# Linear attention and a squared-ReLU FFN on one core: q features scaled as token rows, moved by SBUF transfers, and x taken straight from the num product

## The chip, the cores and the metric

One core of a Trainium2 chip. The metric is device time in microseconds, as the median of several executions. Times of one comparison come from the same chip, with the kernel before run in the same rounds. TensorE multiplies matrices, VectorE and GpSimd work elementwise, ScalarE evaluates activations, SyncE issues transfers.

## The reference

```python
def _attn_ref(q, k, v, S1, S2):               # batch 4, heads 4, seq 1088, head_dim 32, r = 8
    def phi(x):
        a = np.einsum('rd,bhsd->bhsr', S1, x)
        b = np.einsum('rd,bhsd->bhsr', S2, x)
        return np.einsum('bhsi,bhsj->bhsij', a, b).reshape(*x.shape[:-1], r * r)
    q_p, k_p = (phi(q), phi(k))
    kv = np.einsum('bhsf,bhsd->bhfd', k_p, v)
    z = np.sum(k_p, axis=2)
    num = np.einsum('bhsf,bhfd->bhsd', q_p, kv)
    den = np.einsum('bhsf,bhf->bhs', q_p, z)[..., None] + 1e-06
    return (num / den).astype(np.float32)

def _moe_ref(x, w_in, w_out):                 # x: 4352 x 128, w_in: 128 x 2048
    h = np.maximum(x @ w_in, 0.0)
    return (h * h @ w_out).astype(np.float32)
```

## The kernel before

The FFN runs as one long stream on TensorE: 12 chunks (4 batches of 3, with 384, 384 and 320 tokens), each of 16 steps. A step is one f16 product (pg, 128 tokens of d_ff wide), a relu (gt) and a square (g) on ScalarE, VectorE or GpSimd, and one f32 product that accumulates in po. The attention of the next chunk is woven into this stream: a planner puts each small task into a step, and the tasks of a step are issued in that order on their engines, which work through their queues in order.

The k features of a batch are turned into token rows (fs) and multiplied with one another (kp), half on VectorE and half on GpSimd:

```python
    def a_fs(b, g):
        ...
            nc.vector.transpose(fs[:, 0 : 32 * n], kf[:, 0 : 32 * n])

    def a_kp2(b, g):
        fs = st[b, "fs", g]
        ...
        (nc.vector if g == 0 else nc.gpsimd).tensor_tensor(
            out=_ap(st[b, "kp2"], 0, 128, 128 * NT * g, [[64, 2 * NT], [8, 8], [1, 8]]),
            in0=_ap(fs, 0, 128, 0, [[16, 2 * NT], [2, 8], [0, 8]]),
            in1=_ap(fs, 0, 128, 1, [[16, 2 * NT], [0, 8], [2, 8]]),
            op=mult,
        )

    def k_tasks(n):
        for g in range(2):
            P.add(("fs", n, g), "DVE", 0.45, [("kf", n)], a_fs, n, g)
        ...
        for g in range(2):
            P.add(("kp", n, g), ("DVE", "POOL")[g], (1.36, 3.15)[g], [("fs", n, g)], a_kp2, n, g)
        turn_q(n, 0)
```

The q features of a chunk (a_qg) are spread by four VectorE shuffles and multiplied by GpSimd (qp). One group of products (a_ndn) makes num and den, and VectorE divides:

```python
    def a_ndn(b, ch):
        ...
        for i in range(2):               # num, den
            for g in range(2):
                for h in range(H):
                    nc.tensor.matmul(nd[32*h : 32*h+32, 512*g + 192*i : ...],
                                     kw[64*g : 64*g+64, 128*i + 32*h : ...], qpn[64*g : ...])
    # then: dT = transpose(den); de = dT + 1e-6; rd = 1 / de; rb = transpose(rd); x = num * rb
```

## Time and profile before

| | before |
|---|---|
| time, median of 3 runs | 195.05 us (194.82 to 195.51) |
| profiled span | 193.2 us |
| TensorE, ScalarE, VectorE, GpSimd busy | 96, 71, 64, 49% |
| first FFN product of po starts | 18.6 us |

In a page the busy share says how long an engine had something in flight; the slices show where. In a timeline the columns are start, length, engine, source line, operation and tiles; a bracket gives the idle time before it and who ended it. Two groups of the page are the halves of kp (count, then busy us, mean ns, idle before):

```profile
L306 POOL TENSOR_TENSOR kp<-fs 128x1152 f32<-128x1152 f32 x3 | 9.5, 3169 | 5.0 <-DVE fs L299 5.0
L306 DVE TENSOR_TENSOR kp<-fs 128x1152 f32<-128x1152 f32 x3 | 3.9, 1316 | 0.0
```

### The profile page before, as it was taken

How to read it: one execution, taken by the hardware profiler on the slowest of the kernel's cores; microseconds unless marked ns; L12 is line 12 of the kernel's file. 1: busy time of each engine (PE TensorE's matmuls, PEld its weight loads, DVE VectorE, ACT ScalarE, POOL GpSimd, SP SyncE). 2: the span in 40 equal slices, each digit the busy share in tenths (PEclk: the TensorE clock that was granted, in tenths of full speed). 3: DMA queues.
4: the chain of work that ended last, by engine and by line, in shares of the span. 5: the costliest groups of instructions: out<-in, count | busy, mean ns of one | idle time of the engine just before them, and what ended most of it. 6: DMA issues, size and time to landing. Idle time of an engine off the chain costs nothing.

```text
span 193.2 us, 4586 instructions
## 1 busy us (share of the span) xinstructions
PE 185.9 (96%) x1666; PEld 111.2 (58%) x1666; DVE 122.8 (64%) x316; ACT 138.1 (71%) x338; POOL 94.7 (49%) x158
## 2 busy tenths in 40 slices
PE   7998999999999999999999999999999999999990
PEld 2673655456656555456666555556566555556990
DVE  3958876974586763964566674873666665547740
ACT  3326695895496996996498896896596896867740
POOL 5833484955325382984346363984245371630000
PEclk9999999999999999999999999999999999999997
DMA  5699340020085100020157200010110200200201
GB/s 163 177 289 299 88 142 5 0 41 3 12 204 155 43 11 3 11 33 3 17 154 210 38 6 3 14 29 3 25 19 2 34 3 0 41 2 0 44 0 34
DMA packets 27344, 11.40 MB, mean 59 GB/s; under 512 B 19194, under 2 KB 26042, under 8 KB 27322
## 3 DMA queue, kind: packets, MB, share of 16 engines
q1 hardware_dynamic: 27174, 11.05, 23.5%
q8 instruction: 13, 0.21, 0.5%
q10 hardware_dynamic: 148, 0.07, 0.1%
q14 instruction: 9, 0.07, 0.1%
HBM read 8.78 MB, written 2.23 MB: 57 GB/s over the span
## 4 chain that ended last, share of the span: by engine, by line
PE 93%; DVE 2%; ACT 2%; issue 0%; DVEq 0%; ACTq 0%
PE po L756 58%; PE pg L725 16%; PE ndn L472 4%; PE kvp L338 2%; PE warm L877 2%; PE qg L441 2%; PE pt L773 2%; PE nd L595 2%; PE rep L901 1%; PE kvp L352 1%; PE sm L522 1%; PE kf L381 1%; PE kf L280 1%; ACT gt L735 1%; ACT g L719 1%
## 5 line engine op out<-in xcount | busy, mean ns | idle before, releaser
L756 PE MATMUL po<-g,w_o 128*128 128x384 f32 (+3 forms) x386 | 144.0, 459 | 0.0
L719 ACT ACTIVATE g<-gt 128x384 f32<-128x384 f32 (+1 forms) x164 | 80.7, 503 | 7.7 <-DVE gt L737 7.1
L735 ACT ACTIVATE gt<-pg 128x384 f32<-128x384 f32 (+2 forms) x137 | 64.6, 474 | 28.6 <-PE pg L725 27.9
L756 PEld LDWEIGHTS po<-g,w_o 128*128 128x128 f32 x386 | 65.9, 190 | 32.7 <-ACT g L719 18.7
L725 PE MATMUL pg<-xT,w_in 128*128 128x384 f16 (+2 forms) x193 | 60.9, 317 | 0.7 <-ACT xT L697 0.3
L737 DVE TENSOR_SCALAR gt<-pg 128x384 f32<-128x384 f32 (+1 forms) x56 | 29.4, 524 | 34.4 <-PE pg L725 27.9
L746 POOL TENSOR_TENSOR g<-gt 128x384 f32<-128x384 f32 (+1 forms) x26 | 20.7, 801 | 49.0 <-ACT gt L735 49.0
L725 PEld LDWEIGHTS <-w_in 128*128 128x128 f16 x193 | 18.9, 98 | 24.4 <-issue 6.8
L459 POOL TENSOR_TENSOR qp<-sh 128x384 f32<-128x384 f32 (+1 forms) x20 | 18.8, 948 | 7.9 <-DVE sh L450 7.9
L450 DVE STREAM_SHUFFLE sh<-qg 128x384 f32<-128x384 f32 (+1 forms) x40 | 20.4, 563 | 0.0
L546 POOL TENSOR_TENSOR xT<-x,rs 128x384 f16<-128x384 f32 (+1 forms) x10 | 9.5, 952 | 6.2 <-DVE rs L537 6.0
L306 POOL TENSOR_TENSOR kp<-fs 128x1152 f32<-128x1152 f32 x3 | 9.5, 3169 | 5.0 <-DVE fs L299 5.0
L537 DVE TENSOR_SCALAR rs<-sm 128x384 uint32<-128x384 uint32 (+1 forms) x10 | 5.3, 527 | 7.9 <-PE sm L522 7.9
L482 DVE STREAM_TRANSPOSE dT<-ndn 128x384 f32<-128x384 f32 (+1 forms) x10 | 5.5, 548 | 7.0 <-PE ndn L472 7.0
L788 POOL COPY br<-beta 32x3 f32<-32x3 f32 x32 | 5.9, 183 | 6.4 <-DVE beta L678 5.1
L472 PE MATMUL ndn<-qp,kw 64*32 64x192 f32 (+1 forms) x320 | 8.4, 318 | 0.0
L555 POOL TENSOR_TENSOR bt<-s 128x384 f32<-128x384 f32 (+1 forms) x10 | 7.9, 786 | 0.0
L472 PEld LDWEIGHTS ndn<-qp,kw 64*32 64x32 f32 x320 | 4.7, 106 | 4.9 <-issue 3.9
L364 POOL TENSOR_TENSOR ks<-kp 128x1024 f32<-128x1024 f32 x3 | 7.1, 2365 | 0.2
L877 PE MATMUL warm<-zero 128*128 128x512 f16 x16 | 5.7, 521 | 1.2 <-DVE zero L160 1.2
L338 PEld LDWEIGHTS kvp<-kp,vn 128*32 128x32 f32 x288 | 4.8, 110 | 2.7 <-issue 2.2
L274 DVE STREAM_TRANSPOSE qT<-qn 128x384 f32<-128x384 f32 (+1 forms) x12 | 6.3, 535 | 0.0
(119 smaller groups left out, 154.9 us busy)
## 6 DMA issues: line engine op xcount, KB each, us to landing
vn<-in_v_dram SPq DMA_DIRECT2D x32, 64.0 KB, 3.9
kn<-in_k_dram SPq DMA_DIRECT2D x3, 544.0 KB, 11.9
qn<-in_q_dram SPq DMA_DIRECT2D x3, 544.0 KB, 3.3
out_dram<-oT SPq DMA_DIRECT2D x24, 48.0 KB, 1.8
w_in<-in_moe_w_in_dram SPq DMA_DIRECT2D x2, 512.0 KB, 9.0
w_o<-in_moe_w_out_dram SPq DMA_DIRECT2D x2, 512.0 KB, 11.1
out_dram<-oT SPq DMA_DIRECT2D x12, 40.0 KB, 1.7
qn<-in_q_dram SPq DMA_DIRECT2D x2, 192.0 KB, 3.8
```

The lines of the kernel that those rows point to most:

```text
L306: (nc.vector if g == 0 else nc.gpsimd).tensor_tensor(out=_ap(st[b, "kp2"], 0, 128, 128 * NT * g, [[64, 2 * NT], [8, 8], [1, 8]]), in0=_ap( ...
L450: nc.vector.stream_shuffle(in_=_ap(st[b, "qg", ch], 0, 128, 0, [[512, 2], [1, n]]), out=_ap(t_, 0, 128, 0, [[n, 2], [1, n]]), mask=mask_q[ ...
L459: nc.gpsimd.tensor_tensor(out=qp[:, 0 : 2 * n], in0=st[b, "sh", ch, s, 0][:, 0 : 2 * n], in1=st[b, "sh", ch, s, 1][:, 0 : 2 * n], op=mult,)
L472: nc.tensor.matmul(nd[32 * h : 32 * h + 32, 512 * g + 192 * i : 512 * g + 192 * i + n], st[b, "kw"][64 * g : 64 * g + 64, 128 * i + 32 * h ...
L546: nc.gpsimd.tensor_tensor(out=st[b, "xT"][:, 384 * ch : 384 * ch + n], in0=st[b, "x", ch][:, 0:n], in1=st[b, "rs", ch][:, 0:n], op=mult,)
L719: nc.scalar.activation(dst, src, Square)
L725: nc.tensor.matmul(pg[:, c0:c1], w_in[:, 128 * c : 128 * c + 128], st[b, "xT"][:, 384 * ch + c0 : 384 * ch + c1],)
L735: nc.scalar.activation(gt[:, c0:c1], pg[:, c0:c1], Relu)
L737: nc.vector.tensor_scalar(out=gt[:, c0:c1], in0=pg[:, c0:c1], scalar1=0.0, scalar2=None, op0=amax)
L746: (nc.vector if on[1] == "DVE" else nc.gpsimd).tensor_tensor(out=g2[:, c0:c1], in0=gt[:, c0:c1], in1=gt[:, c0:c1], op=mult)
L756: nc.tensor.matmul(st["po", b, ch][:, c0:c1], w_o[:, 128 * c : 128 * c + 128], g2s[i][1][:, c0:c1], start=first, stop=(c == NFF - 1), skip ...
L877: nc.tensor.matmul(t_[:, 0:512], zero[:, 0:128], zero[:, :])
```

## The change

Its intent is to halve the num and den products on TensorE. The q features are turned into token rows, den is formed there, and one factor is scaled by 1/den, so that the num product gives x directly. Turned back, half of the feature rows lie on the wrong partitions and are moved by SBUF transfers. Since z is no longer multiplied on TensorE for these chunks, the ones products go and a gram product (a_gram) of the k features takes their place, for which fs gets a new layout. The core of the diff, with cuts marked:

```diff
     def a_fs(b, g):
...
-            nc.vector.transpose(fs[:, 0 : 32 * n], kf[:, 0 : 32 * n])
+            nc.vector.transpose(
+                _ap(st[b, "fs"], 0, 128, 2 * g, [[32, 2 * NT], [4, 8], [1, 2]]),
+                _ap(kf, 0, 128, 0, [[16, 2 * NT], [2, 8], [1, 2]]),
+            )
...
     def a_kp2(b, g):
...
-            in0=_ap(fs, 0, 128, 0, [[16, 2 * NT], [2, 8], [0, 8]]),
-            in1=_ap(fs, 0, 128, 1, [[16, 2 * NT], [0, 8], [2, 8]]),
+            in0=_ap(fs, 0, 128, 2 * g, [[32, 2 * NT], [4, 8], [0, 8]]),
+            in1=_ap(fs, 0, 128, 2 * g + 1, [[32, 2 * NT], [0, 8], [4, 8]]),
...
+    def a_qgy(b, ch, qg):
...
+        for r in range(2):
+            for g in range(2):
...
+                nc.tensor.matmul(qg[64 * g : 64 * g + 64, ...], sw[b % 2][64 * r : 64 * r + 64, :], ...)
...
+    def a_mv(b, ch, e):
...
+        for to, p_, c_, of, o_ in todo:
+            nc.sync.dma_start(_ap(to, p_, 32, c_, [[1, n]]), _ap(of, o_, 32, 0, [[1, n]]))
...
     def feature_tasks(b, ch):
...
+        P.add(("tq", b, ch), "DVE", 0.5, need, a_tq, b, ch)
...
+        P.add(("den", b, ch), "DVE", 1.1, [("tq", b, ch)], a_den, b, ch, lag=0)
+        for e in range(2):
+            P.add(("qp2", b, ch, e), "POOL", 1.05, [("den", b, ch)], a_qp2, b, ch, e)
+        for e in range(2):
+            P.add(("bk", b, ch, e), "DVE", 0.5, [("qp2", b, ch, e)], a_bk, b, ch, e)
+            P.add(("mv", b, ch, e), "SP", 0.0, [("bk", b, ch, e)], a_mv, b, ch, e)
+        P.at["mv", b, ch, 1] += 5
...
     def k_tasks(n):
...
-        for g in range(2):
-            P.add(("kp", n, g), ("DVE", "POOL")[g], (1.36, 3.15)[g], [("fs", n, g)], a_kp2, n, g)
-        turn_q(n, 0)
+        P.add(("kp", n, 1), "POOL", 3.15, [("fs", n, 1)], a_kp2, n, 1)
+        if n == 1:
+            x_tasks(0, 2)
+        P.add(("kp", n, 0), "DVE", 1.36, [("fs", n, 0)], a_kp2, n, 0, slow=n > 1 and 1.5)
```

## The prediction

> **What bounds the kernel now.** I read the page first, then the chain that ended last, then the longest waits, then the timeline of TensorE alone. From the page, busy shares and the slices:
>
> ```profile
> PE 185.9 (96%) x1666; PEld 111.2 (58%) x1666; DVE 122.8 (64%) x316; ACT 138.1 (71%) x338; POOL 94.7 (49%) x158
> ...
> PE   7998999999999999999999999999999999999990
> ...
> PE 93%; DVE 2%; ACT 2%; issue 0%; DVEq 0%; ACTq 0%
> ```
>
> TensorE is busy 96% of 193.2 us, at 90% or more in all slices from the fifth to the last but one, and 93% of the chain that ended last is its own work; no other engine passes 71%. A busy TensorE need not be a full one, so I checked its timeline. Columns: start, length, work.
>
> ```profile
> 104.61 0.70 PE L756 MATMUL po<-g,w_o 128*128 128x320 f32 x2
> 105.24 0.88 PE L472 MATMUL ndn<-qp,kw 64*32 64x192 f32 x32
> 105.91 0.48 PE L441 MATMUL qg<-qT,sqn 64*32 64x160 f32 x16
> 106.33 0.34 PE L725 MATMUL pg<-xT,w_in 128*128 128x384 f16 x1
> ...
> 114.63 0.81 PE L756 MATMUL po<-g,w_o 128*128 128x384 f32 x2
> 115.27 0.33 PE L725 MATMUL pg<-xT,w_in 128*128 128x384 f16 x1
> 115.44 0.81 PE L756 MATMUL po<-g,w_o 128*128 128x384 f32 x2
> ...
> 131.93 1.21 PE L338 MATMUL kvp<-kp,vn 128*32 128x64 f32 x72
> 132.95 0.29 PE L352 MATMUL kvp<-kp,ones 128*32 128x64 f32 x8
> 133.07 0.29 PE L352 MATMUL kvp<-ks,ones 128*32 128x64 f32 x8
> 133.29 0.34 PE L725 MATMUL pg<-xT,w_in 128*128 128x384 f16 x1
> ```
>
> I go by distances between starts, as lengths overlap. A full FFN step takes 115.44 - 114.63 = 0.81 us: 0.64 for the f32 product of 384 columns and 0.17 for the f16 one, that is 600 f32 columns a us and 2400 f16 ones. I walked all starts from 18.6 us to the end and subtracted these rates. Apart from the attention groups, under half a us is left over, around 177.6 to 179.2, where ScalarE is late. So TensorE is full, and the time follows **what is put into its queue**. The waits say the same: the longest belong to engines waiting for work.
>
> ```profile
> POOL g L746 <- ACT gt L735: 49.0, 21, 4.8
> ACT gt L735 <- PE pg L725: 27.9, 40, 1.8
> DVE gt L737 <- PE pg L725: 27.9, 45, 2.0
> ```
>
> The columns are total, count and longest in us. All three are slack on the other engines.
>
> **The Trainium skill.** (1) "TensorEngine Tiling (Array Packing)", section Available Configurations, lists 64x32 as 8 independent tiles and 64x64 as 4. The trace agrees on 64x32: 8 products of qg (192 columns each) take about the time of one, 192/600 = 0.32 us plus an edge. (2) Same page, Key Properties: changing the tiling mode, not just the tile, drains TensorE. The trace fits. Between an FFN po and the ndn start there is 105.24 - 104.61 = 0.63 us, where 320 columns need 0.53: 0.10 us of edge. Out of qg there is 106.33 - 105.91 = 0.42 where 160 columns need 0.27: 0.15 us. Between ndn and qg, both 64*32, the start distance is 0.67 for 2 x 0.32: only 0.03. So a change of mode costs 0.10 to 0.15 us. (3) "DMA: Bandwidth & Descriptors", section Anatomy of one DMA (written for the GpSimd path), puts the fixed cost at about 2.0 us; here, issued by SyncE, output writes of 48 KB land in 1.8 us. (4) "GPSIMD Engine Reference", section Key points, says that GpSimd cannot access PSUM (no run here shows it), which is why xs must leave GpSimd when x is read straight from the num product.
>
> **The change part by part, on TensorE.** Three batches (b = 1 to 3) of three chunks change: six of 192-column and three of 160-column halves. Batch 0 keeps its path.
>
> 1. Num and den products: 16 products a chunk (two rounds of eight tiles) become 8 (one round), as den is applied to the q features beforehand. Two rounds were 0.67 us (192) and 0.57 (160: 117.79 to 118.36), so half: 6 x 0.335 + 3 x 0.285 = **-2.8 us**.
> 2. The q feature product stays one round of the same columns, but is 4 products of 64x64 instead of 8 of 64x32. No column time changes, but by point (2) the num product and the q product no longer share a mode: 8 groups x 0.12 = **+1.0 us**. In two groups the k features (64*32) follow, another 2 x 0.12 = **+0.2**.
> 3. The first q product of batches 2 and 3 was a group of its own (122.38 po to 123.61 pg, 1.23 us, less 0.64 for po: 0.59, where the columns need 0.32). It now rides in another group: two groups' edges of 0.25, **-0.5 us**.
> 4. In the kv group the ones products (8 of 64 columns, two rounds, 0.34 with a tail of 0.12: 0.22) become 9 gram products of 32 columns spread over the column tiles. If each stands alone, 9 x 32/600 = 0.48, so +0.26 a batch; if they hide beside the kv products, -0.2. I take +0.13 x 3 = **+0.4 us**.
> 5. Transposes of kv: batch 0's pair (0.22 us) moves to before the FFN stream begins, where TensorE waits for the first x behind warm-up products; some 0.1 of it may come back there. One of two goes in later batches, but a small product with a mask takes its place. Sum **-0.2 us**.
> 6. The |x| sum splits into two products of 192: 9 x 0.02, **+0.2 us**.
> 7. The last chunk leaves its output-tile products out of steps 0, 1, 6, 11 instead of the first four, which spreads the 0.4 us of lateness at 177.6: **-0.3 us**.
>
> Sum: -2.8 + 1.2 - 0.5 + 0.4 - 0.2 + 0.2 - 0.3 = -2.0 us.
>
> **Off TensorE.** A changed chunk loses on VectorE four shuffles (4 x 0.563), dT 0.548, de and rd 0.59, rb 0.54 and x 0.518: 4.4 us. It gains a turn of the features (about 0.54), four small operations for den (estimate 0.2 to 0.3 each from de and rd, 1.0), two turns back (1.08) and xs (0.52): 3.1 us. So 1.3 us less, 9 times, 12 us of VectorE. GpSimd loses qpn (2 x 0.948) and xs (0.952) a chunk and the ks sums (2.365 + 2 x 1.003 a batch) and gains two products of about 1.0 each: 0.8 a chunk and 4.4 a batch, about 20 us. None of this bounds the span, so its worth is near 0 by itself; it gives the FFN evictions more room. Six SBUF transfers a chunk are added, 54 in all, each 32 rows of 1.5 KB = 48 KB. Their latency lies between the turn back and the num product; the schedule leaves five extra steps plus the usual two, 7 x 0.81 = 5.7 us, against an estimate of 2 to 3 us after the output writes of the same size. I add **+0.4 us** for stalls where they queue behind loads of the next batch (landing 3.3 to 11.9 us in the page) or where a late VectorE turn eats the margin. Total -1.6; 195.05 - 1.6 = 193.4. As this kernel's stream has been kept free of stalls with care and the new schedule spreads its work evenly, I lean a little to the good side: **193.0 us**.
>
> **Rivals.**
> A. *The mode change costs nothing between 64x32 and 64x64* (or only the entry and exit count). Then the 1.2 us stay won: 191.8 us. For it: the 0.03 us between ndn and qg shows groups can run on seamlessly. Against: the 0.10 and 0.15 at both edges of every group.
> B. *The transfers become a new wait on TensorE.* Its queue is in order, so a num product waiting on a late transfer holds the whole FFN. One us in half of the nine chunks gives 4 to 5 us: 197 to 198. For it: one queue carries loads, outputs and moves, in order; the first chunk of batch 1 has the longest chain (k features, kv, gram, q, turn, product, turn back, move). Against: 5.7 us of room.
> C. *VectorE becomes the bound locally*: the new schedule lets it be loaded to 1.25 us a step everywhere where 0.99 held before, and the small den operations come in bursts. For it: an FFN step is only 0.81 us, so late relus would stall po. Against: its total falls by 12 us. It would cost 1 to 2 us: 194 to 195.
> D. *Everything off TensorE is hidden and nothing was on the path*: if the gram and the mode changes are worth more than I take, 194 to 195, no change.
>
> **Range and chances.** Summing the certain gain (2.8 + 0.5 + 0.5) with nothing against it gives 191.3, which I take as the low end. All costs at their high end (1.5 for modes, 0.8 for gram, 1.5 of stalls) against the gains give about 195. More than 2% faster means below 191.1 us, beyond the column arithmetic: 0.12. Slower than 199 needs rival B in most chunks: 0.04. The rest is 0.84.
>
> **What would show each step.** In the changed trace: the num product should have 16 instructions of 64*32 and a start distance of 0.33 us plus an edge; the q product, 64*64, should start 0.10 to 0.15 us later than the columns of num alone need (step 2; if 0.03, rival A). The kv group with its grams should take 1.4 to 1.7 us from po's end to the next pg (1.45 now). The gap at 177.6 should shrink. VectorE should fall to about 110 us and GpSimd to about 75, less what the FFN is given from ScalarE. Rival B would show as TensorE idle before ndn ended by a DMA; rival C as idle before po ended by VectorE. The prediction is wrong if those waits sum to over 2 us, or if the packed products do not share the array as they do now.

## The result and the profile after

The changed kernel takes 201.61 us (200.76 to 203.14, 4 runs) against 195.13 us for the kernel before in the same rounds. The ratio is 1.034, with a 95% interval from 1.027 to 1.041. Ratios here are the mean time of one kernel's fast runs over that of the other's fast runs of the same rounds, so not quite the ratio of the medians. A run over 1.5% above the fastest of the same kernel counts as slow. The page after:

```profile
PE 186.3 (94%) x1468; PEld 108.4 (54%) x1468; DVE 123.5 (62%) x284; ACT 130.6 (66%) x322; POOL 85.0 (43%) x166
...
PE   7997999899999699999999599999999999999990
...
PEclk9999999999999999999999879999999999999999
...
PE 77%; DVE 9%; issue 4%; DMA 3%; ACT 2%; SPq 2%; POOL 1%; ACTq 0%; DVEq 0%
```

TensorE has holes in the slices from 35, 65 and 110 us (8, 6 and 5; a slice is 5.0 us), and of the chain that ended last its share fell from 93 to 77%. To see where 6.0 us of span went, I split the time after the first po by the distances between the starts of all matmuls. "FFN columns" are the columns of pg, po and pt at 2400 and 600 a us. "Attention" is the distance from each attention matmul to the next one. "Rest" is what the FFN matmuls took beyond their columns: edges of groups (0.10 us each), a few ns per product, and waits. The row doesn't add up to the span: 5.2 us before and 5.6 us after lie behind the start of the last matmul.

| profiled run | first po | FFN columns | attention | rest | span |
|---|---|---|---|---|---|
| before | 18.6 | 144.5 | 20.6 | 4.3 | 193.2 |
| changed | 18.3 | 144.5 | 20.1 | 10.8 | 199.2 |

So attention on TensorE shrank and the FFN stream now waits. The single steps that lose over 0.25 us are few: 1.4 us near 35 us, 2.0 at 65.6, 2.4 at 109.3, and 1.4 in slow products up to 116.5. A num product at 153.6 waits 0.4 us for a transfer. Here is the timeline of the third of them:

```profile
106.76 2.71 POOL L361 TENSOR_TENSOR kp<-fs 128x1152 f32<-128x1152 f32 x1
...
107.16 4.36 DVE L361 TENSOR_TENSOR kp<-fs 128x1152 f32<-128x1152 f32 x1
...
109.24 0.49 ACT L918 ACTIVATE gt<-pg 128x384 f32<-128x384 f32 x1
...
111.42 0.56 DVE L920 TENSOR_SCALAR gt<-pg 128x384 f32<-128x384 f32 x1
...
112.04 0.32 PE L908 MATMUL pg<-xT,w_in 128*128 128x384 f16 x1 [2.25 <-DVE gt L920]
```

VectorE's half of kp, 1.32 us before, is recorded as 4.36 us. It starts 0.40 us after GpSimd's half and ends 2.05 us after that one has ended. The next relu (gt) stands behind it in VectorE's queue, and TensorE waits 2.25 us for that relu. In the kernel before the order was the other way about:

```profile
119.93 1.32 DVE L306 TENSOR_TENSOR kp<-fs 128x1152 f32<-128x1152 f32 x1
120.08 3.19 POOL L306 TENSOR_TENSOR kp<-fs 128x1152 f32<-128x1152 f32 x1 [1.38 <-DVE fs L299]
```

VectorE started first, and GpSimd's half, which nobody was waiting for, ended 2.02 us after VectorE's. The hole near 35 us has the same neighbour, but a tiny instruction on VectorE:

```profile
31.43 2.70 POOL L361 TENSOR_TENSOR kp<-fs 128x1152 f32<-128x1152 f32 x1 [1.31 <-DVE fs L352]
31.78 2.38 DVE L668 TENSOR_SCALAR de<-dT 128x10 f32<-128x10 f32 x1
...
35.40 2.21 DVE L361 TENSOR_TENSOR kp<-fs 128x1152 f32<-128x1152 f32 x1
35.51 0.56 ACT L693 ACTIVATE ax<-x,tiny 128x320 bf16<-128x320 f32 x1 [1.43 <-DVE x L684]
36.12 0.30 PE L701 MATMUL sm<-ax,part 128*128 128x320 bf16 x1 [0.78 <-ACT ax L693]
```

Adding 1e-6 to 10 columns lasts 2.38 us, until GpSimd's kp ends; x, ax and sm follow late, and ScalarE, which stands at ax, does no relus meanwhile. The kp at 35.40, with GpSimd idle, takes 2.21 us: dearer than 1.32 even alone. After the 2.25 us hole TensorE is slow for a while, as the granted clock by stretch shows (after the stretch come busy us and count of TensorE, weight loads, VectorE, ScalarE and GpSimd, then the clock, the DMA share and GB/s):

```profile
109.80:112.00 2.20, 0.00 (x0) 0.00 (x0) 2.20 (x3) 0.00 (x0) 0.00 (x0) 1.00 0.19 45
112.00:113.30 1.30, 1.26 (x5) 0.80 (x5) 1.21 (x3) 0.97 (x3) 0.00 (x0) 1.00 0.00 0
113.30:117.10 3.80, 3.80 (x30) 1.37 (x29) 0.71 (x2) 0.87 (x2) 0.83 (x1) 0.55 0.31 47
```

The clock is 0.55 for 3.8 us, which costs 3.8 x 0.45 = 1.7 us (an estimate from this row). Most of the loss doesn't need it: another of the four runs of the changed kernel had a mean clock of 0.997, where a stretch like this one alone would lower it to 0.991 (1 - 1.7/199), and still took 200.76 us. The 2.0 us hole near 65 us was followed by no low clock.

**Theories.** LOCK: a product of two SBUF tensors, or a short SBUF operation like de, on VectorE can't run beside a GpSimd instruction that reads SBUF; the later one waits for the whole of the other, and the wait is counted as its length. The Trainium skill says so in "SBUF — State Buffer", section SBUF: two separate sides: the pair of ports that the two share is "an exclusive lock, not a bandwidth split", and who starts first has it for the whole instruction. It names two kinds of VectorE operation: those with two SBUF inputs, against a GpSimd operation that reads SBUF (kp is one), and those in what it calls a 2-port perf mode. That de runs in such a mode is an inference; the runs show only that it waited. The traces above agree with the lock (2.05 us and 2.02 us left after the other's end). LAYOUT: kp reads one element in every 16 bytes instead of every 8. The same page, section Specifications (TRN2), gives SBUF lines of 16 bytes of which at least two hits are needed for full bandwidth; 2.21 against 1.32 us would fit. The rivals: TRANSFERS (the new SBUF moves), and COST (kp's own work, with no lock).

### The profile page after: what moved, and what is told of

The parts are those of the page before. It is cut to its first block, busy times and chain, and to the rows that moved or that the text cites. A ratio compares the mean times of both kernels' runs of the same rounds, so it can differ in the third digit from the quotient of the medians.

```text
span 199.2 us, 4283 instructions
## 1 busy us (share of the span) xinstructions
PE 186.3 (94%) x1468; PEld 108.4 (54%) x1468; DVE 123.5 (62%) x284; ACT 130.6 (66%) x322; POOL 85.0 (43%) x166
## 3 DMA queue, kind: packets, MB, share of 16 engines
HBM read 8.80 MB, written 2.23 MB: 55 GB/s over the span
## 4 chain that ended last, share of the span: by engine, by line
PE 77%; DVE 9%; issue 4%; DMA 3%; ACT 2%; SPq 2%; POOL 1%; ACTq 0%; DVEq 0%
PE po L939 48%; PE pg L908 13%; PE kvp L393 3%; PE ndn L637 2%; PE qk L564 2%; PE pt L956 2%; SPq L141 2%; PE nd L778 2%; DMA kn<-in_k_dram 1%; PE rep L1084 1%; DVE de L668 1%; ACT gt L918 1%; DMA ft<-ft 1%; DMA vn<-in_v_dram 1%; DVE fs L352 1%
## 5 line engine op out<-in xcount | busy, mean ns | idle before, releaser
L939 PEld LDWEIGHTS po<-g,w_o 128*128 128x128 f32 x386 | 65.9, 191 | 37.9 <-issue 20.1
L902 ACT ACTIVATE g<-gt 128x384 f32<-128x384 f32 (+1 forms) x146 | 72.2, 506 | 10.4 <-DVE gt L920 10.0
L929 POOL TENSOR_TENSOR g<-gt 128x384 f32<-128x384 f32 (+1 forms) x44 | 34.4, 789 | 57.9 <-ACT gt L918 57.8
L908 PEld LDWEIGHTS <-w_in 128*128 128x128 f16 x193 | 19.2, 99 | 22.9 <-issue 5.1
L599 POOL TENSOR_TENSOR qp<-tq,bs 128x384 f32<-128x384 f32 (+1 forms) x18 | 14.2, 810 | 16.9 <-DVE bs L591 16.9
L573 DVE STREAM_TRANSPOSE tq<-qk 128x384 f32<-128x384 f32 (+1 forms) x9 | 5.0, 561 | 13.7 <-PE qk L564 8.7
L361 DVE TENSOR_TENSOR kp<-fs 128x1152 f32<-128x1152 f32 x3 | 10.9, 3636 | 0.0
L985 DVE SCALAR_TENSOR_TENSOR sc<-po,bt 128x384 f32<-128x384 f32 (+1 forms) x9 | 4.8, 528 | 6.4 <-PE po L939 6.3
L720 DVE TENSOR_SCALAR rs<-ndn 128x384 uint32<-128x384 uint32 (+1 forms) x9 | 4.8, 536 | 3.7 <-PE ndn L704 3.5
L393 PE MATMUL kvp<-kp,vn 128*32 128x64 f32 x288 | 6.5, 223 | 0.0
L956 PE MATMUL pt<-w_o,g 128*128 128x128 f32 x32 | 5.7, 274 | 0.0
L637 PE MATMUL ndn<-ft,kw 64*32 64x192 f32 (+1 forms) x144 | 5.6, 347 | 0.0
```

Of the source, the lines that this page charges most:

```text
L361: (nc.vector if g == 0 else nc.gpsimd).tensor_tensor(out=_ap(st[b, "kp2"], 0, 128, 128 * NT * g, [[64, 2 * NT], [8, 8], [1, 8]]), in0=_ap( ...
L393: nc.tensor.matmul(st[b, "kvp"][32 * h : 32 * h + 32, 0:64], _ap(vn[b], 0, n, v0 + dv * h, [[1, 32]]), kp[0:n, at[h] : at[h] + 64], start= ...
L599: nc.gpsimd.tensor_tensor(out=_ap(qp, 0, 128, 0, [[32, m], [8, 4], [1, 8]]), in0=_ap(st[b, "tq", ch], 0, 128, 4 * e, [[32, m], [1, 4], [0, ...
L637: nc.tensor.matmul(nd[32 * h : 32 * h + 32, 512 * g : 512 * g + n], st[b, "kw"][64 * g : 64 * g + 64, 32 * h : 32 * h + 32], st[b, ch, "ft ...
L902: nc.scalar.activation(dst, src, Square)
L908: nc.tensor.matmul(pg[:, c0:c1], w_in[:, 128 * c : 128 * c + 128], st[b, "xT"][:, 384 * ch + c0 : 384 * ch + c1],)
```

## The experiments

Ten kernels ran, all correct. The first four shared one set of runs of the kernel before (195.4 us), the next four another (195.17 us), the last two a third (195.14 us). One run each of e3, e5 and e8 was slow; it is in the median given, but not in the ratio.

**e1: VectorE's half first.**

```diff
-        P.add(("kp", n, 1), "POOL", 3.15, [("fs", n, 1)], a_kp2, n, 1)
+        P.fix(("kp", n, 0), "DVE", 1.36, P.at["fs", n, 1], a_kp2, n, 0)
+        P.add(("kp", n, 1), "POOL", 3.15, [("fs", n, 1)], a_kp2, n, 1)
         if n == 1:
             x_tasks(0, 2)
-        P.add(("kp", n, 0), "DVE", 1.36, [("fs", n, 0)], a_kp2, n, 0, slow=n > 1 and 1.5)
```

> The changed kernel with one order undone: VectorE's half of the k products (kp) is queued right after the turn fs, ahead of GpSimd's half, as in the kernel before. In the changed kernel GpSimd's half starts first (2.70 us) and VectorE's half, begun 0.40 us later, lasts 4.34 us. Theory LOCK (a product of two SBUF tensors on VectorE waits for the whole of a GpSimd instruction that reads SBUF): VectorE's kp falls to about 2.2 us, GpSimd's kp grows to about 4.5, the stalls of TensorE near 65 and 109 us (2.0 and 2.4 us, and the low clock after the second) go; about 196 us. Rival TRANSFERS (the new SBUF moves hold things up): no change, 201 to 202. Rival COST (kp is slow by itself from its new layout): VectorE's kp stays near 4.3 us and the time at 201.

Measured: 204.23 us, ratio 1.045 (1.038 to 1.052). Slower, where every theory had said 196 or no change. The timeline of batch 1:

```profile
31.99 2.23 DVE L361 TENSOR_TENSOR kp<-fs 128x1152 f32<-128x1152 f32 x1
32.15 4.62 POOL L361 TENSOR_TENSOR kp<-fs 128x1152 f32<-128x1152 f32 x1 [1.31 <-DVE fs L352]
...
34.69 2.11 DVE L668 TENSOR_SCALAR de<-dT 128x10 f32<-128x10 f32 x1
...
38.77 0.42 PE L701 MATMUL sm<-ax,part 128*128 128x320 bf16 x1 [2.70 <-ACT ax L693]
```

The durations are those of LOCK: 2.23 us on VectorE, 4.62 on GpSimd, where 2.70 was its own. But the wait was only handed on. GpSimd's kp now ends at 36.8 instead of 34.1 us, de waits for it again (2.11 us), and sm comes 2.65 us later than in the changed kernel, with the 2.2 us of kp ahead of it; TensorE idles 2.7 us there and then runs at clock 0.50 for 6.3 us (38.77 to 45.09), which costs some 3.2 us (an estimate, half of 6.3). In batches 2 and 3 VectorE's kp meets another GpSimd product (2.73 us), and the x of the running chunk waits behind it (1.9 and 1.4 us). So the order of the two halves alone is no cure; the time forecast of LOCK was wrong, its durations were right.

**e2: 8 byte step.** The order of all instructions is unchanged; only fs stores the two factors in separate halves.

```diff
-                _ap(st[b, "fs"], 0, 128, 2 * g, [[32, 2 * NT], [4, 8], [1, 2]]),
-                _ap(kf, 0, 128, 0, [[16, 2 * NT], [2, 8], [1, 2]]),
+                _ap(st[b, "fs"], 0, 128, g, [[2, 16 * NT], [32 * NT, 2]]),
+                _ap(kf, 0, 128, 0, [[2, 16 * NT], [1, 2]]),
...
-            in0=_ap(fs, 0, 128, 2 * g, [[32, 2 * NT], [4, 8], [0, 8]]),
-            in1=_ap(fs, 0, 128, 2 * g + 1, [[32, 2 * NT], [0, 8], [4, 8]]),
+            in0=_ap(fs, 0, 128, g, [[16, 2 * NT], [2, 8], [0, 8]]),
+            in1=_ap(fs, 0, 128, 32 * NT + g, [[16, 2 * NT], [0, 8], [2, 8]]),
```

(a_gram reads the two halves as contiguous columns.)

> The changed kernel with only the layout of the k features altered, so that each kp reads with a step of 8 bytes as before instead of 16; the order of all instructions is the same. Theory LOCK plus LAYOUT: VectorE's kp without a GpSimd neighbour (batch 1) falls from 2.2 to 1.3 us; with one, from 4.34 to about 3 (the rest of a shorter GpSimd kp of about 2.0, then 1.3); the stalls shrink but do not go; about 197 us. LOCK alone: kp unchanged, 201 to 202. Rival COST (layout alone): kp 1.3 us everywhere and about 194.5. Rival TRANSFERS: no change in time.

Measured: 199.33 us, ratio 1.017 (1.010 to 1.025): slower than the kernel before, but whether by 2% is unclear. The instructions of kp (least, median and most ns):

```profile
L361 POOL TENSOR_TENSOR kp<-fs x3: 2274/2275/2282, 33.9 to 108.1; 128x1152 f32<-128x1152 f32 x3
L361 DVE TENSOR_TENSOR kp<-fs x3: 1348/3094/3099, 37.5 to 108.5; 128x1152 f32<-128x1152 f32 x3
```

Alone, VectorE's half is back at 1.35 us; GpSimd's fell from 2.70 to 2.28; beside GpSimd VectorE's still lasts 3.09. So LAYOUT and LOCK are both there, and COST alone (1.3 us everywhere) falls. The gain of 2.3 us over the changed kernel was half of what the 197 us expected would have been.

**e3: both edits.** Together, the edits of e1 and e2.

> The changed kernel with both: VectorE's kp first and the 8 byte step. LOCK plus LAYOUT: kp 1.3 us on VectorE, about 3.2 on GpSimd, as in the kernel before; the idle of TensorE at the FFN falls from 10.4 us to about 4 (3.3 in the kernel before), and the smaller attention share (20.8 against 22.4 us) shows: 193 to 195 us, near the 193.0 predicted. If transfers are the cause, it stays above 199.

Measured: 201.57 us, ratio 1.028 (1.020 to 1.036), a miss. Its profiled run fell in the slow state, so I read only durations from it: VectorE's kp 1.33 us in batch 1, then de 1.71 us behind GpSimd's, and 1.68 us for VectorE's kp in the other two batches. They fit the reason found in e1; with no fast trace that isn't shown. (The expectation's 10.4, 3.3, 20.8 and 22.4 us come from another way of splitting than the table above.)

**e4: both halves on GpSimd**, in the same places of the plan.

```diff
-        (nc.vector if g == 0 else nc.gpsimd).tensor_tensor(
+        nc.gpsimd.tensor_tensor(
```

> The changed kernel with both halves of kp on GpSimd, in the same places of the plan; VectorE gets none. All other instructions keep their order. LOCK: VectorE loses 10.9 us of kp and the stalls near 65 and 109 us go, though GpSimd's second half is done no sooner (2 x 2.7 = 5.4 us, about when VectorE's is done now); the one at 34 us ([...]de, behind GpSimd's kp) stays: 195 to 196.5 us. If kp's late result were what hurts (kv waiting for it), no change: 201. Rival TRANSFERS: no change.

Measured: 196.28 us, ratio 1.004 (0.998 to 1.010). The holes at 65 and 109 us are gone, that at 35 stays, as LOCK said; the rest falls from 10.8 to 5.9 us. The transfers are all still there, so TRANSFERS can't be what made the change slow.

**e5: the two halves one after the other**, by a real dependence: VectorE writes an element that GpSimd's half then overwrites.

```diff
+        if g == 0:
+            nc.vector.memset(st[b, "kp2"][:, 128 * NT : 128 * NT + 1], 0.0)
...
-        P.add(("kp", n, 1), "POOL", 3.15, [("fs", n, 1)], a_kp2, n, 1)
         if n == 1:
             x_tasks(0, 2)
         P.add(("kp", n, 0), "DVE", 1.36, [("fs", n, 0)], a_kp2, n, 0, slow=n > 1 and 1.5)
+        P.add(("kp", n, 1), "POOL", 3.15, [("kp", n, 0)], a_kp2, n, 1, lag=0)
```

> The changed kernel, 16 byte step kept, but GpSimd's half of kp is made to follow VectorE's by a real dependence (VectorE writes one element of GpSimd's output, which GpSimd then overwrites), so the two never overlap and the short operation de of batch 1 meets no GpSimd kp either. LOCK: VectorE's kp 2.2 us in all three batches, GpSimd's 2.7, de about 0.2 us instead of 2.4; the stalls of TensorE near 35, 66 and 109 us shrink to well under 1 us each; 195 to 197 us. If the lock is not the cause and kp's work as such is, the stalls stay near 2 us and the time above 199.

Measured: 196.18 us (fast runs 195.27 to 196.65), ratio 1.000 (0.992 to 1.008).

```profile
L361 DVE TENSOR_TENSOR kp<-fs x3: 2210/2245/2247, 33.8 to 105.1; 128x1152 f32<-128x1152 f32 x3
L361 POOL TENSOR_TENSOR kp<-fs x3: 2696/2697/2702, 36.2 to 107.4; 128x1152 f32<-128x1152 f32 x3
...
L670 DVE TENSOR_SCALAR de<-dT x1: 175/175/175, 32.4 to 32.4; 128x10 f32<-128x10 f32 x1
```

The work, the layout and the transfers are those of the changed kernel (the plan moved a few relus between engines), and kp has its plain durations in all three batches; de took 0.18 us. Taking away the overlap of the two engines takes away the 3.4%, to within the 0.8% of the interval. The rest falls from 10.8 to 4.8 us. Attention rises to 21.0 us, since two num products wait 1.5 us for transfers.

**e6: the lock in the kernel before.** One swap in each batch, so that GpSimd's half starts first.

```diff
-        for g in range(2):
-            P.add(("kp", n, g), ("DVE", "POOL")[g], (1.36, 3.15)[g], [("fs", n, g)], a_kp2, n, g)
-        turn_q(n, 0)
+        P.add(("kp", n, 1), "POOL", 3.15, [("fs", n, 1)], a_kp2, n, 1)
+        turn_q(n, 0)
+        P.add(("kp", n, 0), "DVE", 1.36, [("fs", n, 0)], a_kp2, n, 0, first=P.at["qT", n, 0])
```

> The kernel BEFORE with one swap in each of batches 1 to 3: VectorE turns q (0.57 us) ahead of its half of kp instead of after, so that GpSimd's half, which needs no more than fs, starts first. Everything else, the 8 byte step too, is as before. LOCK: VectorE's kp grows from 1.32 us to about 2.9 (the rest of a 2.0 us kp on GpSimd, then 1.3), GpSimd's shrinks from 3.17 to about 2.0 (it waited for VectorE before); the kernel gets slower by 0.5 to 4 us as relus queue behind kp. Without a lock both durations stay and the time is 195.

Measured: 196.79 us, ratio 1.0065 (1.001 to 1.012).

```profile
L306 POOL TENSOR_TENSOR kp<-fs x3: 2165/2165/2167, 32.5 to 120.7; 128x1152 f32<-128x1152 f32 x3
L306 DVE TENSOR_TENSOR kp<-fs x3: 2745/3074/3077, 33.1 to 121.0; 128x1152 f32<-128x1152 f32 x3
```

The lengths change places: GpSimd 3.17 to 2.17, VectorE 1.32 to 3.07. None of the change is in this kernel, so the lock is the chip's and not the change's. The cost in time is small: this trace has two holes of about 0.5 us where the changed kernel has three of 1.4 to 2.4. Why they are shorter was not tested.

**e7: the changed kernel repaired.** Both halves on GpSimd (e4), the 8 byte step (e2), and in batch 0's third chunk 1e-6 is added while den is read from PSUM, in place of de.

```diff
-        nc.vector.transpose(_ap(dT, ...), _ap(st[b, "nd", ch], 0, 128, 192, [[512, 2], [1, n]]))
+        nc.vector.tensor_scalar(out=_ap(dn, ...), in0=_ap(st[b, "nd", ch], 0, 128, 192, [[512, 2], [1, n]]),
+                                scalar1=1e-6, scalar2=None, op0=add)
+        nc.vector.transpose(dT[:, 0 : 2 * n], dn[:, 0 : 2 * n])
```

> The changed kernel with both halves of kp on GpSimd, the 8 byte step, and the den of batch 0's third chunk with its 1e-6 added while it is read from PSUM (so de, which waited 2.4 us for GpSimd, is gone). LOCK plus LAYOUT: GpSimd's kp 2.0 us each, no VectorE instruction over 0.8 us beside it, the stall near 35 us gone; idle at the FFN back to some 4.3 us as in the kernel before; 193 to 194.5 us. If it stays at 196, something else of the change costs.

Measured: 195.63 us, ratio 1.001 (0.994 to 1.008), above the 193 to 194.5 expected. GpSimd's halves took 2.28 us each. The rest is 4.29 us, as in the kernel before, and the hole at 35 us is gone. Yet the time only equals the kernel before. Its num products of two chunks took 0.81 and 1.12 us instead of 0.48, waiting for transfers: 1.0 us. The first po came 0.4 us later than in the kernel before, with no cause that I could show.

**e8: the q product in the num product's mode.**

```diff
-            for g in range(2):
-                c0 = 384 * ch + n * g
+            for o in range(4):
+                c0 = 384 * ch + n * (o // 2)
                 nc.tensor.matmul(
-                    qg[64 * g : 64 * g + 64, 512 * r : 512 * r + n],
-                    sw[b % 2][64 * r : 64 * r + 64, :],
+                    qg[32 * o : 32 * o + 32, 512 * r : 512 * r + n],
+                    sw[b % 2][64 * r : 64 * r + 64, 32 * (o % 2) : 32 * (o % 2) + 32],
```

> The same repaired kernel with the q feature product as 8 products of 64x32 instead of 4 of 64x64, so that it shares its tiling mode with the num product before it and the k features after it. MODE CHANGE (0.12 to 0.14 us each, 8 + 2 of them): 1.2 us less, 192 to 193 us, and the num product's distance to the q product falls from 0.48 to about 0.35 us. Rival A of the prediction (a change between these two modes is free): no difference.

Measured: 194.39 us (fast runs 193.5 to 194.72), ratio 0.993 (0.987 to 0.999), above the 192 to 193 expected. A group of TensorE in the changed kernel, then the same in this one:

```profile
56.03 0.56 PE L637 MATMUL ndn<-ft,kw 64*32 64x192 f32 x16
56.52 0.56 PE L564 MATMUL qk<-qT,sw 64*64 64x192 f32 x8
57.01 0.72 PE L431 MATMUL qk<-kq,sk 64*32 64x288 f32 x16
```

```profile
55.31 0.56 PE L637 MATMUL ndn<-ft,kw 64*32 64x192 f32 x16
55.66 0.53 PE L564 MATMUL qk<-qT,sw 64*32 64x192 f32 x16
55.98 0.69 PE L431 MATMUL qk<-kq,sk 64*32 64x288 f32 x16
```

From start to start 0.49 became 0.35 and 0.49 became 0.32, with twice the instructions in the q product. By these distances the ten changes of mode cost 8 x 0.14 + 2 x 0.17 = 1.5 us. Attention on TensorE fell from 19.97 us in e7 to 18.79, by the 1.2 us expected; it would have been 1.5, but two num products of this trace wait for transfers, some 1.3 us in all against 1.0 in e7. Rival A of the prediction falls. One of these two shows why they wait:

```profile
61.60 1.15 SPq L626 DMA_DIRECT2D ft<-ft  x2
62.88 3.71 SPq L626 DMA_DIRECT2D ft<-u  x4
...
67.36 1.10 PE L637 MATMUL ndn<-ft,kw 64*32 64x192 f32 x12
68.12 0.34 PE L564 MATMUL qk<-qT,sw 64*32 64x160 f32 x4
```

The moves themselves land in 1.9 us in the median and 2.7 at most here. But SyncE issues the six of a chunk one after the other, and from the first issue to the last it takes 3.1 to 4.5 us in this trace (4.5 for this chunk). With the landing that is 5.0 to 6.4 us. Why some single issues take 1.5 us where the median is 0.54 was not tested.

**e10: e8 again in five rounds.**

> The repaired kernel with the 64x32 q product once more, in five rounds, to narrow the interval against the kernel before (0.9929, from 0.9865 to 0.9993, in three rounds): the traces say 1.5 us less (191.7 against 193.2 us of span), so a ratio of 0.990 to 0.995.

Measured: 194.3 us (193.01 to 195.19), ratio 0.995 (0.992 to 0.998), at the upper edge of what was expected. The spread of over 2 us would fit waits for transfers that come and go (in this trace two num products still waited); with one trace that isn't shown.

**e9: two more steps for the transfers.**

```diff
-        P.at["mv", b, ch, 1] += 5
+        P.at["mv", b, ch, 1] += 5 if (b, ch) == (1, 0) else 7
```

> The same with the num product planned two steps later behind the transfers, 7 steps instead of 5 for all chunks but the first of batch 1 (which has no room). In the repaired kernels the num products of two chunks still waited for a transfer, 0.4 and 0.3 us in one trace, 0.3 and 0.6 in the other. If those waits are the transfers alone, they go and the time falls by about 0.7 us; if not, other work of the plan moves and it stays within 0.5 us of the run beside it.

Measured: 192.1 us (191.99 to 193.41), ratio 0.986 (0.984 to 0.988): below the kernel before by 1.4%, clear of the interval though less than 2%, and by 2.2 us below e10 beside it, more than the 0.7 expected. No num product waits in its trace: each takes 0.35 us at 192 columns before a q product, and attention is 17.4 us, 1.6 less than in e10's trace. The profiled run, 193.41 us, lost some 1.2 us to half-speed products between 19.1 and 21.7 us, which is about what sets it off from the other runs at 192. What the plan moved besides the num products was not separated.

## Why the prediction was wrong

193.0 us was predicted, in a range of 191.3 to 195; 201.61 was measured. By its own steps:

- **What bounds the kernel** was right for the kernel before: TensorE is full, and the FFN columns stay at 144.5 us in every trace. One reading was too low: apart from attention not "under half a us" but 4.3 us is left over before, 1.7 of it in edges and 2.6 in a few ns per product; only 0.3 us is a wait. The miss doesn't come from there.
- **Step 1**, -2.8 us: held. In e8's trace the num products that don't wait take 0.35 and 0.30 us, where they were 0.67 and 0.57 with den: 6 x 0.32 + 3 x 0.27 = 2.7.
- **Step 2**, +1.2 us for changes of mode: held in kind and a little low; the distances in e7 and e8 give 1.5.
- **Step 3**, -0.5 us: the two separate q groups are gone from the trace.
- **Step 4**, +0.4 us: too high. The kv group takes 1.38 us (39.37 to 40.75) with the grams, 1.37 us before, so they add nothing beside the kv products.
- **Steps 5 and 6**: near, -0.1 and 0.0 us. **Step 7**, -0.3: the lateness at the last chunk is gone.
- **The step that failed** is "I add +0.4 us for stalls", in the part off TensorE. In the changed trace the stalls are some 7.6 us (1.4 + 2.0 + 2.4 + 1.4 + 0.4), 5.8 us of them behind VectorE operations that waited for GpSimd. The prediction's own sign of being wrong, such waits of over 2 us in sum, came true: 4.1 us of idle before pg ended by VectorE (it had named po). The mechanism of these stalls was missing too: the list of what VectorE and GpSimd gain and lose left out kp, which the diff shows twice, once with a new step and once with the halves in the other order. "About 12 us of VectorE" saved came out as 0.7 us more busy time: kp grew from 3.9 to 10.9 us and de by 2.2, mostly waits for GpSimd, which are counted as busy. The 12 was too much by itself, though: e5, without these waits, has 118.4 us, 4.4 less than before, and of the gap only the slower layout of kp (2.8 us) is traced.
- **Rival C** (VectorE the local bound, 1 to 2 us) named the right engine and the wrong reason: not the bursts of small operations, but a queue held up by another engine. **Rival B** (transfers) was real at a tenth of its size in the changed kernel, 0.4 us, and 1.0 to 1.6 us in e5, e7, e8 and e10. The estimate of 2 to 3 us against 5.7 us of room counted the landing of one transfer and not the six issues in a row: 5.0 to 6.4 us in e8's trace.

The 6 us between the two kernels are thus the lock with the longer kp behind it, and, in the profiled run, the clock that falls after the longest hole. e5 shows that taking away the overlap takes away the loss. What the layout alone costs is the step from the changed kernel to e2, about 2 us, measured with the lock in force. The low clock is the 1.7 us estimated above; no experiment isolated it, and the run of 200.76 us went without it.

## What to carry to other kernels

When a change reorders elementwise work, list every instruction of VectorE and GpSimd that may run side by side, and ask which starts first: an instruction that nobody waits for may hold one that the whole pipeline stands behind. An instruction whose recorded length varies with its neighbour, like the 3.17 us of GpSimd's kp before, is a warning to be read before predicting. Keep neighbouring groups of small matmuls in one tiling mode even at twice the instructions, and when several transfers feed one product, add up their issues on the queue, here six of 0.5 to 1.7 us each, and not only the landing of one.

## What the Trainium skill lacked or had wrong

- "SBUF — State Buffer" has the lock but not that a profile counts the wait as length of the waiter: a 10-column operation of 0.18 us was recorded as 2.38 us, a 1.32 us product as 3.07.
- The same page speaks of a penalty but gives no cost for VectorE with one hit in a 16 byte line: the product of 1152 elements rose from 1.35 to 2.21 us there.
- "TensorEngine Tiling (Array Packing)" says that a change of mode drains TensorE without a number: 0.14 to 0.17 us between 64x32 and 64x64 here.
- "TensorE: Matmul & The Clock Gate", section Why this matters for your kernels, warns of idle gaps over about 3 us; here a hole of 2.25 us was followed by a granted clock of 0.55 for 3.8 us, starting 1.3 us after work resumed, and one of 2.7 us in e1 by 0.50 for 6.3 us.
- "DMA: Bandwidth & Descriptors", section Anatomy of one DMA (written for the GpSimd path; SyncE issues here), calls HBM the heaviest target: SBUF to SBUF transfers of 48 KB landed in 1.9 us in the median (3.6 at most), no sooner than the 1.9 us of output writes of that size.
